# An adaLN block with linear attention and a GEGLU FFN: the 1/den broadcast loads dealt over two DMA queues, and the w_mod loads of the second gate placed behind the KV transposes

## The chip, the cores and the metric

One core of a Trainium2 chip runs the whole kernel. The metric is device microseconds (us) of one execution, as the median over several runs. The kernel before takes 805.02 us (three runs, 804.95 to 805.1).

The core has a matmul engine (PE, with its weight loads listed apart as PEld), a vector engine (DVE), a scalar engine (ACT), GpSimd (POOL), and a sync engine (SP) that does nothing here but issue DMAs. A DMA issued from SP or from ACT stands in that engine's instruction stream: it waits there for its semaphores, and what is behind it in the stream waits too.

## The reference

The input x is 2048 x 1024 in bf16. Six modulation rows come from one matrix product; they scale and shift the two normalised inputs and gate the two branches.

```python
mod = (_silu(c) @ w_mod).reshape(c.shape[0], 6, 1, -1)
sa, ca, ga, sb, cb, gb = (mod[:, 0], ..., mod[:, 5])
h = _layernorm(x) * (1 + ca) + sa
x = x + ga * _A_ref(h, A_wqkv, A_wo)        # linear attention, 32 heads of 32
h = _layernorm(x) * (1 + cb) + sb
x = x + gb * _B_ref(h, B_w_gate, B_w_up, B_w_down)   # gelu(h@wg) * (h@wu) @ wd, F = 3584
```

In the attention, with `phi(t) = where(t > 0, t + 1, exp(t)) + 1e-6`:

```python
pq, pk = phi(q), phi(k)
kv  = einsum('bhsd,bhse->bhde', pk, v);  z = einsum('bhsd->bhd', pk)
num = einsum('bhqd,bhde->bhqe', pq, kv)
den = einsum('bhqd,bhd->bhq', pq, z)[..., None] + 1e-6
o = num / den          # then @ wo
```

## The kernel before, in words

The 2048 rows are 16 chunks of 128 rows, in 4 supergroups (`sg`) of 512 rows. The 32 heads are 8 groups `g` of 4 heads `k`; each head holds 32 of the 128 partitions. The work goes through these stages on PE:

- **K and Q** (lines 858 and 909, to about 128 us): products of the modulated input with the weights; ACT and DVE make `phi` of them.
- **M tiles** (`m_tile`, line 873, from 127.8 us). Values are never formed: `M = phi(k)^T x` is made instead, in 24 tiles numbered `n`, each about 2.3 us of PE. A group has three tiles; `mcp` on ACT copies each to `mb` (line 878). When a group is complete, `m_t(g)` transposes `mb` to `mtb` by a DMA from SP (line 678), and `kv_prod(g)` (line 891) multiplies that with the value weights. `w2_pair` then folds the output weights in. The groups 0 to 3 become complete with tiles 2, 5, 8 and 11, and their `kv_prod` comes after the tiles 6, 9, 12 and 15.
- **den and its inverse.** `den` (line 1201) makes the denominators of two supergroups; DVE inverts them (line 1207) and SP stores them to DRAM in `scr_rd` (line 1209). `rb_load(sg, (h,))` (line 1221) reads them back for the half `h` (256 rows) of a supergroup, spread from one row per head to that head's 32 partitions: four DMAs of 256 KB, one for each quarter `k` of the partitions, together 1 MB in `rb`. `pq_scale` (line 1234, DVE, four instructions per half) multiplies `phi(q)` with it.
- **The output product** (`wo_chunk`, line 1242, chunks 0 to 15 from 193.8 us), 16 matmuls of 0.216 us to a chunk. DVE adds it to x (lines 1251 and 1255); ACT and POOL make the second normalisation (`ln2_stats` and `ln2_rows`: two ACT passes per chunk, lines 649 and 637), and a DMA transpose from SP gives `h2a` and `h2b` (line 678). For chunks 2 to 13 the work beside a chunk is in a hand-written table `SLOT`: `rb_load(2, (0,))` in slot 2, `(2, (1,))` in 4, `(3, (0,))` in 5, `(3, (1,))` in 10. `wt_dma` loads the first FFN weights (line 1325), `x_dma` reloads rows of x (line 569).
- **The FFN** (lines 1411 and 1496) in two passes, from about 246 us to the end. It multiplies by sums and differences of operand blocks (`ss` on line 1366, `tp` on line 1386) that DVE makes.

Beside the M tiles DVE also makes modulation rows from w_mod. `mod_step`, three times to a tile, does one multiply-add: 48 of them read `wmst` (loads on line 572), then `gb_acc` does 16 for the last half of the second gate `gb`, which read `wmg`. `gb_load(j, q)` (line 761) loads `wmg`: 512 KB each, `j` the column block of 512 columns, `q` the half of the rows; there are two buffers, so `gb_load(1, q)` waits until DVE has read `gb_load(0, q)`.

Everything is first listed in program order; the order on PE and SP is that order. `reorder` then plans the order on DVE, ACT and POOL anew, with a table of costs and due times, for the stretch from the end of the first K products up to slot 2; after that the written order holds. Each DMA issuer has a number of semaphore lanes (`LANES`), used in turn; a DMA waits until the one before it on its lane has landed.

The load of one half, before:

```python
for k in range(HPG):
    made.append(sch.dma(Q, lambda e, h=h, k=k: e.dma_start(
        RB[i][32 * k:32 * (k + 1), h, :, :],
        scr_rd[sg, h, k:k + 1, :, :].to_broadcast([32, NG, HW])), ...
```

`Q` is SP's stream, `A` is ACT's, `NG` is 8 and `HW` is 256 values of 4 bytes. In DRAM the 8 rows of 1 KB are 64 bytes apart (`SGW // 2 + 16`).

Of the kernel before, what the change touches and what calls it, by code (L numbers as in the profile page):

```python
# [14 lines left out]
NSG = 4  # L15
CPG = NCH // NSG
SGW = P * CPG
NDC = D // P
NG = 8
HPG = 4  # L20
# [8 lines left out]
PE_, ACT_, DVE_, POOL_, SP_ = "PE", "ACT", "DVE", "POOL", "SP"  # L29
# [124 lines left out]
class Sched:  # L154


    LANES = {SP_: 8, POOL_: 4, ACT_: 2}

    def __init__(self):
        self.streams = {e: [] for e in ENGS}  # L160
# [35 lines left out]
    def dma(self, stream, fn, rd=(), wr=(), deps=(), note="", overwrite_ok=False):  # L196
        nl = self.LANES[stream]
        k = self.lane_rr.get(stream, 0)
        self.lane_rr[stream] = (k + 1) % nl
        lane = f"{stream}q{k}"  # L200
        dd = list(deps)
        prev = self.lane_last.get(lane)
        if prev is not None:
            dd.append(prev)
        o = self.op(stream, fn, rd=rd, wr=wr, deps=dd, dma_lane=lane, note=note, overwrite_ok=overwrite_ok)
        self.lane_last[lane] = o
        return o
# [106 lines left out]
def bass_adaLN_cond__linear_attn_block__geglu_ffn__prompt_kernel(  # L314
# [12 lines left out]
    bf16, f32, f32r, i32 = dt.bfloat16, dt.float32, dt.float32r, dt.int32  # L327
    scr_row = nc.dram_tensor("scr_row", [3, 4, 512], f32).ap()
    scr_mod = nc.dram_tensor("scr_mod", [2, NDC, P], f32).ap()
    scr_rd = nc.dram_tensor("scr_rd", [NSG, 2, HPG, NG, SGW // 2 + 16], f32).ap()[:, :, :, :, 0:SGW // 2]  # L330
    with ExitStack() as es:
        es.enter_context(nc.allow_non_contiguous_dma(reason="1024 modulation values, laid out by partition"))
        arena = es.enter_context(nc.sbuf_tensor("arena", [P, ARENA_BYTES], dt.uint8, align_bytes=64))
# [4 lines left out]
        def at(name, shape, dty, off):  # L338
            return nc.alloc_sbuf_tensor_at(name, shape, dty, offset=ABASE + off, align_bytes=4)
# [33 lines left out]
        RB = [at(f"rb{i}", [P, 2, NG, SGW // 2], f32, OFF_RB[i]) for i in range(2)]  # L373
# [6 lines left out]
        GBB = at("gbb", [P, D], f32, OFF_GBB)  # L380
# [40 lines left out]
        def r_sm(name):  # L421
            return [(SMO[name], SMO[name] + SMSZ[name], name)]
# [7 lines left out]
        def r_xs(c0, c1):  # L430
            return [t_ for c_ in range(c0, c1) for t_ in r_x(c_)]
# [30 lines left out]
        def r_h2(h, k0=0, k1=NDC, s0=0, s1=SGW):  # L462
            return r_t8(H2O[h], f"h2{'ab'[h]}", k0, k1, s0, s1)
# [37 lines left out]
        def r_rb(i, h, g0=0, g1=NG):  # L501
            return [(OFF_RB[i] + (h * NG + g0) * 1024, OFF_RB[i] + (h * NG + g1) * 1024, f"rb{i}")]
# [12 lines left out]
        R_GBB = [(OFF_GBB, OFF_GBB + 4096, "gbb")]  # L515
# [13 lines left out]
        sch = Sched()  # L529
        T, A, V, G, Q = PE_, ACT_, DVE_, POOL_, SP_  # L530
# [37 lines left out]
        def x_dma(c0, c1):  # L568
            return sch.dma(Q, lambda e: e.dma_start(XALL[:, c0:c1, :], x_v[:, c0:c1, :]), wr=r_xs(c0, c1), note=f"x{c0}")
# [123 lines left out]
        def h2ap(h, dc, s0, s1):  # L693
            return H2[h][:, dc, s0:s1]
# [20 lines left out]
        def sc2(dc):  # L715
            return CB1T[:, dc:dc + 1], SBT[:, dc:dc + 1], r_sm("cb1T") + r_sm("sbT")
# [8 lines left out]
        def mod2_act(h, c0=0, n=CPG, dc0=0, dc1=NDC):  # L725
            s0, s1 = c0 * P, (c0 + n) * P
            for dc in range(dc0, dc1):
                sA, sB, rs_ = sc2(dc)
                sch.op(A, lambda e, dc=dc, sA=sA, sB=sB: e.activation(h2ap(h, dc, s0, s1), h2ap(h, dc, s0, s1), ACTF.Identity, bias=sB, scale=sA),
                       rd=r_h2(h, dc, dc + 1, s0, s1) + rs_, wr=r_h2(h, dc, dc + 1, s0, s1), note=f"h2modb {h}.{dc}")  # L730
# [29 lines left out]
        def gb_load(j, q):  # L760
            sch.dma(Q, lambda e: e.dma_start(WMG[q][:], wm_v[:, 4 * q:4 * q + 4, (10 + j) * 512:(11 + j) * 512]), wr=r_wmg(q), note=f"wmg{j}.{q}")
# [6 lines left out]
        def gb_acc(j, dc):  # L768
            acc, rng = GA_[j]
            src, rs_ = WMG[dc // 4][:, dc % 4, :], r_wmg(dc // 4, dc % 4, dc % 4 + 1) + r_sm("silf")  # L770
            if dc == 0:
                sch.op(V, lambda e: e.tensor_scalar(acc[:, :], src, SILF[:, 0:1], None, op0=ALU.mult), rd=rs_, wr=rng, note=f"macc{6 + j}.0")
            else:
                sch.op(V, lambda e: e.scalar_tensor_tensor(acc[:, :], src, SILF[:, dc:dc + 1], acc[:, :], op0=ALU.mult, op1=ALU.add),
                       rd=rs_ + rng, wr=rng, note=f"macc{6 + j}.{dc}")
            if dc % 4 == 3 and j == 0:
                gb_load(1, dc // 4)

        def gb_hilo(j):
            acc, rng = GA_[j]  # L780
# [3 lines left out]
        o_gb = [None]  # L784
# [47 lines left out]
        def row_load(dst, rng, row, a0, note, o_):  # L832
            sch.dma(Q, lambda e: e.dma_start(dst[:, :].rearrange("p (a b) -> p a b", a=2),
                                             scr_row[row, a0:a0 + 2, :].rearrange("(o a) b -> o a b", o=1).to_broadcast([P, 2, 512])),
                    wr=rng, deps=[o_], note=note)
# [281 lines left out]
        for c_ in range(10, NCH):  # L1117
            b = seq.index(("k", c_ // 2 * 2, 0)) - (9 if c_ % 2 else 12)
# [6 lines left out]
        for c_ in range(8, NCH, 2):  # L1125
            b = seq.index(("k", c_, 0)) - 3
# [10 lines left out]
        for g in range(NG):  # L1137
            task(nk + g // 2, lambda g=g: sch.dma(Q, lambda e: e.dma_start(WV[:, g, :, :], wqkv_v[:, :, 2 * D + g * P:2 * D + (g + 1) * P]),
                                                  wr=r_wv(g), note=f"wv{g}"))
# [54 lines left out]
        HW = SGW // 2  # L1194
# [18 lines left out]
        o_rd = {}  # L1213
        rb_ops = {}

        def rb_load(sg, hs=(0, 1)):
            i = sg % 2
            for h in hs:
                made = []
                for k in range(HPG):  # L1220
                    made.append(sch.dma(Q, lambda e, h=h, k=k: e.dma_start(  # L1221
                        RB[i][32 * k:32 * (k + 1), h, :, :],
                        scr_rd[sg, h, k:k + 1, :, :].to_broadcast([32, NG, HW])),
                        wr=r_rb(i, h) if k == 0 else (), deps=made[0].deps if k else [o_rd[sg // 2]], note=f"rb{sg}.{h}.{k}"))
                rb_ops[sg, h] = made

        GH = [((0, 2), (2, 4)), ((4, 6), (6, 8))]

        def pq_scale(sg, h, gs):
            i, t0 = sg % 2, h * HW  # L1230
            for g0, g1 in gs:
                ap = PQ[sg][:, g0:g1, t0:t0 + HW]
                rng = r_pq(sg, g0, g1, t0, t0 + HW)
                sch.op(V, lambda e, ap=ap, i=i, h=h, g0=g0, g1=g1: e.tensor_tensor(ap, ap, RB[i][:, h, g0:g1, :], ALU.mult),  # L1234
                       rd=rng + r_rb(i, h, g0, g1), wr=rng, deps=rb_ops[sg, h], note=f"pqs{sg}.{h}.{g0}")
# [50 lines left out]
        for n, (g, k) in enumerate(tiles):  # L1286
            m_tile(g, k, n % 4, n % 2)
            if k == 2:
                m_t(g)
            for _ in range(3):  # L1290
                mod_step()
            if 2 <= n <= 9:
                wofold(n - 2)
            while pend and n > 1:
                wm_dma(*pend.pop(0))
            if n in (1, 2):
                gb_load(0, n - 1)
            for f in HOOK.get(n, "").split():
                hook_run(f)
        for i in range(4):  # L1300
# [21 lines left out]
        def wt_dma(u):  # L1322
            i, f0 = u % 2, u * 256
            for t, v_ in enumerate((wg_v, wu_v)):
                sch.dma(Q, lambda e, t=t, v_=v_: e.dma_start(WT[i][:, t, :, :], v_[:, :, f0:f0 + 256]), wr=r_wt(i, t, t + 1), note=f"wt{t} u{u}")
# [20 lines left out]
        ND2 = NDC // 2  # L1346
# [24 lines left out]
        def t_sum(u, k):  # L1371
            if k == 3:
                ap, rd = wq(u, 1, 1)
                for t in range(2):
                    sch.op(A, lambda e, t=t: e.activation(TP[3][:, t, :, :], ap[:, t, :, :], ACTF.Copy), rd=rd[t:t + 1], wr=r_tp(3, t, t + 1), note=f"brcp u{u}")
                return
            if k == 0:
                (in0, r0), (in1, r1) = wq(u, 0, 1), wq(u, 0, 0)
            elif k == 1:
                (in0, r0), (in1, r1) = wq(u, 1, 1), (T32[0], r_tp(0))  # L1380
            elif k == 2:
                (in0, r0), (in1, r1) = wq(u, 1, 1), wq(u, 0, 1)
            else:
                (in0, r0), (in1, r1) = wq(u, 1, 0), (T32[1], r_tp(1))
            for t in range(2):
                sch.op(V, lambda e, t=t: e.tensor_tensor(TP[k][:, t, :, :], in0[:, t, :, :], in1[:, t, :, :], ALU.subtract),  # L1386
                       rd=r0[t:t + 1] + (r1[t:t + 1] if len(r1) == 2 else [(r1[0][0] + t * 2048, r1[0][0] + (t + 1) * 2048, r1[0][2])]),
                       wr=r_tp(k, t, t + 1), note=f"tsum{k} u{u}")
# [123 lines left out]
        def cb1():  # L1512
# [6 lines left out]
                6: lambda: (mod2(0, 0, 2), x_dma(10, 12)),  # L1519
                7: lambda: (t_sum(0, 0), t_sum(0, 1), pq_scale(2, 1, GH[0] + GH[1]), x_dma(12, 14)),  # L1520
                8: lambda: mod2(0, 2, 2),
                9: lambda: (pq_scale(3, 0, GH[0] + GH[1]), t_sum(0, 3), mod2_act(1, 0, 2), mod2_act(1, 2, 2, ND2)),
                10: lambda: (t_sum(0, 4), t_sum(0, 2), rb_load(3, (1,)), x_dma(14, 16), row_load(GBB, R_GBB, 2, 0, "gbb", o_gb[0]), wt_dma(1)),
                11: lambda: None,
                12: lambda: (s_sum(0, 0, 0), mod2(1, 2, 2, 0, ND2)),
                13: lambda: (s_sum(0, 0, 1), s_sum(0, 1, 0), s_sum(0, 1, 1), pq_scale(3, 1, GH[0] + GH[1]), s_sum(0, 2, 0))}
# [142 lines left out]
```

## Time and profile before

| | |
|---|---|
| median of the runs | 805.02 us |
| profiled execution: its own time | 806.37 us |
| profiled execution: span from the first instruction to the last | 804.5 us |
| granted TensorE clock | 1.000 |
| PE, DVE, ACT, POOL busy | 792.9, 568.1, 303.1, 39.4 us |
| loads of `rb`: number, size, median from issue to landing | 32, 256 KB, 5.4 us |
| loads of `wmg`: number, size, median from issue to landing | 4, 512 KB, 6.0 us |
| transposes to `mtb`: number, median and longest to landing | 8, 5.1 and 10.3 us |

The profile shows one execution. An engine row in the timeline gives the start, the duration, the line and operation, the tiles written and read, and in brackets the idle time before it with what ended that idle time. Of an SP or ACT row of a DMA the duration is that of the issue, not of the transfer; the transfer lands later. A row of the windows gives, for a stretch of time, the busy time of each engine, the clock, the busy share of the 16 DMA engines and the rate in GB/s.

### The profile page before, as it was taken

What the parts mean: (1) busy time and instruction counts of PE and PEld (TensorE: products, weight loads), DVE (VectorE), ACT (ScalarE), POOL (GpSimd) and SP (SyncE); (2) the same over time, 40 slices, a digit from 0 to 9 for tenths busy, and PEclk for the clock granted to TensorE, in tenths of its full rate; (3) what the DMA queues carried; (4) which work ended last, traced back from release to release, by engine and by line L of the source; (5) the groups of instructions that cost most, each with busy time, mean ns of one, the idle gap of its engine ahead of it and who ended that gap; (6) DMA issues with size and microseconds to landing.
All of it is one profiled execution on the core that took longest, in us unless ns stands there. A gap on an engine that the chain in (4) does not pass through costs nothing.

```text
span 804.5 us, 10875 instructions
## 1 busy us (share of the span) xinstructions
PE 792.9 (99%) x4029; PEld 465.3 (58%) x4029; DVE 568.1 (71%) x1008; ACT 303.1 (38%) x511; POOL 39.4 (5%) x102
## 2 busy tenths in 40 slices
PE   7999999999999999999999999999999999999998
PEld 4444445666444677767775444467776777744445
DVE  6699898984699978788786375577887878601422
ACT  2497743232655444344443410033544435300000
POOL 2121200000320000000000000000000000000000
PEclk9999999999999999999999999999999999999999
DMA  9789859749898135323237324022231323430100
GB/s 282 242 176 231 176 116 230 186 98 184 186 265 225 53 112 150 98 61 104 58 101 235 53 74 110 20 86 76 82 105 53 106 72 86 136 126 7 53 20 27
DMA packets 168508, 97.73 MB, mean 121 GB/s; under 512 B 68476, under 2 KB 156804, under 8 KB 168456
## 3 DMA queue, kind: packets, MB, share of 16 engines
q1 hardware_dynamic: 168440, 97.04, 47.0%
q8 instruction: 32, 0.52, 0.3%
q14 instruction: 20, 0.16, 0.1%
q10 hardware_dynamic: 16, 0.00, 0.0%
HBM read 78.92 MB, written 4.47 MB: 104 GB/s over the span
## 4 chain that ended last, share of the span: by engine, by line
PE 84%; DMA 6%; SPq 4%; DVE 3%; issue 1%; ACT 1%; POOL 0%; DVEq 0%; POOLq 0%; ACTq 0%
PE ps_all L1411 43%; PE ps_all L1496 24%; PE ps_all L909 7%; PE ps_all L858 6%; PE ps_all L873 3%; DMA rb<-scr_rd 3%; DMA mtb<-mb 1%; SPq L575 1%; DVE pq L1234 1%; DMA wmq<-in_w_mod_dram 1%; SPq L580 1%; DVE ss L1366 1%; SPq L1221 1%; DMA scr_row<-mrowa 1%; SPq L678 1%
## 5 line engine op out<-in xcount | busy, mean ns | idle before, releaser
L1411 PE MATMUL ps_all<-ss,tp 128*128 128x512 f32 x896 | 224.7, 402 | 1.2 <-DVE ss L1366 1.2
L1496 PE MATMUL ps_all<-wd,yT 128*128 128x512 bf16 (+3 forms) x952 | 193.9, 366 | 0.0
L1411 PEld LDWEIGHTS ps_all<-ss,tp 128*128 128x128 f32 x896 | 168.2, 188 | 42.4 <-DVE ss L1366 2.6
L1496 PEld LDWEIGHTS ps_all<-wd,yT 128*128 128x128 bf16 x952 | 90.0, 98 | 103.8 <-ACT ge L1427 0.5
L1427 ACT ACTIVATE ge<-ps_all 128x512 f32<-128x512 f32 x112 | 64.2, 597 | 144.7 <-DVE ps_all L1422 79.7
L1411 PE MATMUL ps_all<-h2a,wt 128*128 128x512 bf16 x448 | 106.2, 380 | 0.4 <-DVE xall L1255 0.4
L1386 DVE TENSOR_TENSOR tp<-wt 128x512 fp32r<-128x512 bf16 x112 | 74.3, 688 | 39.6 <-PE ps_all L1411 20.8
L1431 DVE TENSOR_TENSOR yT<-ge,ps_all 128x512 bf16<-128x512 f32 x112 | 74.7, 685 | 34.4 <-PE ps_all L1411 31.0
L1422 DVE TENSOR_TENSOR ps_all<-ps_all,es 128x512 f32<-128x512 f32 x112 | 75.3, 696 | 16.1 <-PE ps_all L1411 16.1
L1488 DVE TENSOR_TENSOR ps_all<-ps_all,gbb 128x512 f32<-128x512 f32 (+3 forms) x34 | 22.7, 668 | 79.0 <-PE ps_all L1496 79.0
L1386 DVE TENSOR_TENSOR tp<-wt,tp 128x512 fp32r<-128x512 bf16 x112 | 72.0, 684 | 0.0
L1411 PEld LDWEIGHTS ps_all<-h2a,wt 128*128 128x128 bf16 x448 | 39.4, 98 | 55.0 <-issue 14.8
L1242 PE MATMUL ps_all<-w,pq 128*128 128x512 bf16 x256 | 56.5, 379 | 1.6 <-DVE pq L1234 1.6
L858 PE MATMUL ps_all<-wk,h1T 128*128 128x512 bf16 x248 | 56.8, 379 | 0.3 <-DVE h1T L699 0.2
L909 PE MATMUL ps_all<-h1T,wq 128*128 128x512 bf16 x256 | 56.7, 379 | 0.0
L1411 PE MATMUL ps_all<-ar,tp 128*128 128x512 f32 x224 | 55.3, 389 | 0.0
L1416 ACT ACTIVATE ps_all<-ps_all 128x512 f32<-128x512 f32 x56 | 32.6, 582 | 53.2 <-PE ps_all L1411 51.4
L847 ACT ACTIVATE eb<-ps_all 128x512 f32<-128x512 f32 x64 | 36.4, 594 | 37.7 <-PE ps_all L858 15.6
L1411 PEld LDWEIGHTS ps_all<-ar,tp 128*128 128x128 f32 x224 | 42.0, 188 | 8.7
L1242 PEld LDWEIGHTS ps_all<-w,pq 128*128 128x128 bf16 x256 | 24.7, 98 | 32.0 <-DVE pq L1234 2.3
L909 PEld LDWEIGHTS ps_all<-h1T,wq 128*128 128x128 bf16 x256 | 24.9, 98 | 30.0
L1419 ACT ACTIVATE es<-ps_all 128x512 f32<-128x512 f32 x56 | 33.5, 601 | 18.6 <-PE ps_all L1411 18.6
(118 smaller groups left out, 638.0 us busy)
## 6 DMA issues: line engine op xcount, KB each, us to landing
wt<-in_B_w_gate_dram SPq DMA_DIRECT2D x28, 512.0 KB, 4.2
wt<-in_B_w_up_dram SPq DMA_DIRECT2D x28, 512.0 KB, 4.9
wd<-in_B_w_down_dram SPq DMA_DIRECT2D x12, 1024.0 KB, 7.3
rb<-scr_rd SPq DMA_DIRECT2D x32, 256.0 KB, 5.4
wmst<-in_w_mod_dram SPq DMA_DIRECT2D x6, 1024.0 KB, 5.6
wmq<-in_w_mod_dram SPq DMA_DIRECT2D x8, 512.0 KB, 6.1
out_dram<-xall SPq DMA_DIRECT2D x31, 128.0 KB, 1.7
xall<-in_A_x_dram SPq DMA_DIRECT2D x5, 512.0 KB, 4.1
```

The source lines that it names most:

```text
L847: sch.op(A, lambda e: e.activation(EB[i][:, :], PS(bank), ACTF.Exp), prd=pr(bank), wr=rng, note=f"{note}.exp")
L858: o = sch.op(T, lambda e, dc=dc: e.matmul(PS(bank), H1[sg][:, ci, dc, :], W_[:, dc, jg * 512:(jg + 1) * 512], start=(dc == 0), stop=(dc == ...
L909: o = sch.op(T, lambda e, dc=dc: e.matmul(PS(b), WQ[:, dc, qc * P:(qc + 1) * P], H1[sg][:, :, dc, :], start=(dc == 0), stop=(dc == NDC - 1 ...
L1242: last[half] = sch.op(T, lambda e, g=g, half=half: e.matmul(PS(b0 + half), PQ[sg][:, g, ci * P:(ci + 1) * P], W2[:, g, half * 512:(half + ...
L1386: sch.op(V, lambda e, t=t: e.tensor_tensor(TP[k][:, t, :, :], in0[:, t, :, :], in1[:, t, :, :], ALU.subtract), rd=r0[t:t + 1] + (r1[t:t + ...
L1411: o = sch.op(T, lambda e, l_=l_, r_=r_, dc=dc: e.matmul(PS(b), l_, r_, start=fresh and dc == 0, stop=dc == ND2 - 1, skip_group_check=True) ...
L1416: sch.op(A, lambda e: e.activation(PS(BB + t), PS(BA + t), ACTF.Copy), prd=pr(BA + t), pwr=pr(BB + t), note="pcp")
L1419: sch.op(A, lambda e: e.activation(ES[t][:, :], PS(BE + t), ACTF.Copy), prd=pr(BE + t), wr=r_2k(OFF_ES[t], f"es{t}"), note="escp")
L1422: sch.op(V, lambda e: e.tensor_tensor(PS(dst + t), PS(BB + t), ES[t][:, :], ALU.add), prd=pr(BB + t), rd=r_2k(OFF_ES[t], f"es{t}"), pwr=pr ...
L1427: sch.op(A, lambda e: e.activation(GE[i][:, :], PS(b), ACTF.Gelu_apprx_tanh), prd=pr(b), wr=r_2k(OFF_GE[i], f"ge{i}"), note="gelu")
L1431: sch.op(V, lambda e: e.tensor_tensor(YT[:, yrow(fc), h * SGW:(h + 1) * SGW], GE[i][:, :], PS(b + 1), ALU.mult), rd=r_2k(OFF_GE[i], f"ge{i ...
L1496: o = sch.op(T, lambda e, fc=fc: e.matmul(PS(b, 0, n), YT[:, yrow(fc), ci * P:(ci + 1) * P], WDT[fc // 4][:, fc % 4, c0:c1], start=first a ...
```

## The change

It does five things.

1. The four quarter loads of each half of `rb` are issued in the order k = 0, 2, 1, 3, with 0 and 1 from SP and 2 and 3 from ACT, instead of 0, 1, 2, 3 from SP.
2. The padding of 64 bytes behind each 1 KB row of `scr_rd` goes, and both sides of a load are written as one run of 8 KB per partition.
3. ACT gets 8 semaphore lanes for its DMAs instead of 2.
4. `gb_load(0, 0)` and `(0, 1)` move from the M tiles 1 and 2 to the tiles 6 and 7. `gb_load(1, 0)` and `(1, 1)`, issued before as soon as `gb_acc` had listed the last read of each buffer (in tiles 10 and 11), both come at the end of tile 11, behind the transpose of group 3.
5. `rb_load(3, (1,))` moves from the middle of slot 10 to the head of slot 9.

```diff
-    LANES = {SP_: 8, POOL_: 4, ACT_: 2}
+    LANES = {SP_: 8, POOL_: 4, ACT_: 8}
...
-    scr_rd = nc.dram_tensor("scr_rd", [NSG, 2, HPG, NG, SGW // 2 + 16], f32).ap()[:, :, :, :, 0:SGW // 2]
+    scr_rd = nc.dram_tensor("scr_rd", [NSG, 2, HPG, NG, SGW // 2], f32).ap()
...
-            if dc % 4 == 3 and j == 0:
-                gb_load(1, dc // 4)
...
-                for k in range(HPG):
-                    made.append(sch.dma(Q, lambda e, h=h, k=k: e.dma_start(
-                        RB[i][32 * k:32 * (k + 1), h, :, :],
-                        scr_rd[sg, h, k:k + 1, :, :].to_broadcast([32, NG, HW])),
-                        wr=r_rb(i, h) if k == 0 else (), deps=made[0].deps if k else [o_rd[sg // 2]], note=f"rb{sg}.{h}.{k}"))
+                for k in (0, 2, 1, 3):
+                    made.append(sch.dma((Q, A)[k // 2], lambda e, h=h, k=k: e.dma_start(
+                        RB[i][32 * k:32 * (k + 1), h, :, :].rearrange("p a b -> p (a b)"),
+                        scr_rd[sg, h, k:k + 1, :, :].rearrange("k g t -> k (g t)").to_broadcast([32, NG * HW])),
+                        wr=r_rb(i, h) if not made else (), deps=made[0].deps if made else [o_rd[sg // 2]], note=f"rb{sg}.{h}.{k}"))
...
-            if n in (1, 2):
-                gb_load(0, n - 1)
+            if n in (6, 7):
+                gb_load(0, n - 6)
+            if n == 11:
+                gb_load(1, 0)
+                gb_load(1, 1)
...
-                9: lambda: (pq_scale(3, 0, GH[0] + GH[1]), t_sum(0, 3), mod2_act(1, 0, 2), mod2_act(1, 2, 2, ND2)),
-                10: lambda: (t_sum(0, 4), t_sum(0, 2), rb_load(3, (1,)), x_dma(14, 16), row_load(GBB, R_GBB, 2, 0, "gbb", o_gb[0]), wt_dma(1)),
+                9: lambda: (rb_load(3, (1,)), pq_scale(3, 0, GH[0] + GH[1]), t_sum(0, 3), mod2_act(1, 0, 2), mod2_act(1, 2, 2, ND2)),
+                10: lambda: (t_sum(0, 4), t_sum(0, 2), x_dma(14, 16), row_load(GBB, R_GBB, 2, 0, "gbb", o_gb[0]), wt_dma(1)),
```

## The prediction

> **What bounds the kernel now.** I read the page's busy times first, then what PE waited for after the start, then the timelines of PE, DVE and SP around each wait.
>
> ```profile
> PE 792.9 (99%) x4029; PEld 465.3 (58%) x4029; DVE 568.1 (71%) x1008; ACT 303.1 (38%) x511; POOL 39.4 (5%) x102
> ```
>
> PE is busy for 792.9 of 804.5 us, so no edit outside PE's own work can give more than 11.6 us. What it waits for from 27 us on:
>
> ```profile
> PE ps_all L1242 <- DVE pq L1234: 1.6, 1, 1.6
> PE ps_all L1411 <- DVE ss L1366: 1.2, 3, 0.7
> PE ps_all L891 <- DMA mtb<-mb: 1.1, 1, 1.1
> PE ps_all L1411 <- DVE xall L1255: 0.4, 1, 0.4
> ```
>
> That is 4.3 us in all, and it is the ceiling of this change: its loads start after 127 us. Two rows of PE's timeline place the larger waits:
>
> ```profile
> 153.58 0.62 PE L891 MATMUL ps_all<-mtb,wv 128*128 128x128 bf16 x8 [1.11 <-DMA mtb<-mb]
> 231.87 13.99 PE L1242 MATMUL ps_all<-w,pq 128*128 128x512 bf16 x64 [1.59 <-DVE pq L1234]
> ```
>
> For the first, SP's timeline:
>
> ```profile
> 136.83 0.42 SPq L761 DMA_DIRECT2D wmg<-in_w_mod_dram  x1
> 137.35 1.28 SPq L678 DMA_TRANSPOSE mtb<-mb  x1
> 138.73 0.52 SPq L572 DMA_DIRECT2D wmst<-in_w_mod_dram  x1
> 139.30 3.31 SPq L761 DMA_DIRECT2D wmg<-in_w_mod_dram  x1
> 142.71 0.45 SPq L572 DMA_DIRECT2D wmst<-in_w_mod_dram  x1
> 143.26 9.25 SPq L678 DMA_TRANSPOSE mtb<-mb  x2
> ```
>
> The transpose of group 1 is issued at 143.26 and lands 10.3 us later (the longest of its kind; the median is 5.1), behind two `wmg` and two `wmst` loads, 3 MB. For the second wait, DVE's timeline:
>
> ```profile
> 220.73 2.50 DVE L1234 TENSOR_TENSOR pq<-pq,rb 128x512 bf16<-128x512 bf16 x4 [3.00 <-DMA rb<-scr_rd]
> 231.12 2.50 DVE L1234 TENSOR_TENSOR pq<-pq,rb 128x512 bf16<-128x512 bf16 x4 [1.14 <-DMA rb<-scr_rd]
> ```
>
> DVE stood 3.00 and 1.14 us for the two halves of `rb` of supergroup 2. From 231.12 until the FFN runs it is never idle for long, and the small PE waits on `ss` and `xall` (0.44, 0.72, 0.17 and 0.30 us between 246 and 259) are the end of that DVE chain. So the end moves with the landing of the second half, at 231.0. Why these loads are slow is in the windows:
>
> ```profile
> 144.00:150.00 6.00, 6.00 (x48) 4.05 (x46) 6.00 (x8) 1.17 (x4) 0.00 (x0) 1.00 1.10 348
> 197.00:206.00 9.00, 9.00 (x49) 4.22 (x48) 2.17 (x5) 2.05 (x2) 0.19 (x1) 1.00 1.09 218
> 137.60:139.00 1.40, 1.40 (x12) 0.94 (x10) 1.37 (x4) 1.03 (x3) 0.00 (x0) 1.00 1.06 234
> ```
>
> In the first only w_mod loads move (128 partitions, rows of 1 KB): 348 GB/s. In the second only `rb` (32 partitions to a DMA, rows of 1 KB): 218, with the DMA engines as busy. The row length is the same, so it is the 32 partitions or the repeated source. The third is `gab`, a row of 4 KB spread to all 128 partitions: 234.
>
> **The change part by part.**
>
> **First-gate-half loads behind the transpose.** `gb_load(0, .)` leaves the queue ahead of group 1's transpose: 1 MB, at 348 GB/s 3.0 us. The transpose lands at about 150.5 instead of 153.5; PE wants it at 152.47. The wait of 1.11 us goes, with 1.9 us to spare. The other end is no gain, if the first `wmst` transfer still holds the queue. What the loads now stand before: the transpose of group 2. It was ready for PE by 155 at the latest, and its product starts at 161.44; 3.0 us more is covered. The first DVE read of `wmg` is at 158.90; issued near 144.5 and landing after 9.0 (its longest), the load is there at 153.5. I take 1.1.
>
> **Second-block loads behind group 3's transpose.** `gb_load(1, 0)` stood at 163.44, waiting for DVE's fourth `gb_acc`, and group 3's transpose went out behind it at 163.92. Now the transpose goes first; PE took its result at 169.93 without a wait. Nothing is gained. Behind the two loads stand the row store of 169.12 and later the store of 1/den, as the second load did before. Taken at 0.
>
> **The planner.** With other SP positions it may order DVE and ACT differently from 27 us on. PE has no wait there now except the one above; one DVE instruction moved ahead of another costs at most a `wofold` (1.15 us) either way. Taken at 0, bounds -1.2 and +1.2.
>
> **The quarter loads.** SP issues two instead of four to a half, at 0.45 us: 0.9 us less on SP. ACT issues two: 0.9 us by SP's median, 1.2 by the one ACT issue in the trace (0.585). Supergroup 0 and 1: `rb` was not the last wait of PE there (DVE waited 0.51 and 1.74, but PE ran on), so 0. Supergroup 2, first half: issued at 213.13, landed at 220.7, 7.55 us, of which 1 MB at 218 GB/s is 4.8. ACT's two loads follow its normalisation pass that ends at 211.7, so they have 1.4 us of lead. If the two queues together make 348, about 0.49 MB is moved by the lead and 1.6 us remain: landing 213.1 + 2.7 + 1.6 = 217.4. At 234 it is 218.9. DVE is free at 217.73. Its wait of 3.0 falls to between 0 and 1.2.
>
> Second half: from there DVE has 2.4 (`pq_scale`) + 1.1 + 2.1 + 1.2 + 2.5 us of work, so its next `pq_scale` could start near 227.5 to 228.5. In the queues, before the last byte of this half, lie 1 MB of `rb` for each of the two halves, 1 MB of `wt` (3.6 us at 295 GB/s, the rate of the window from 253 to 255, where `wt` moves), three transposes (3.8 us by their issue rows of 1.25), and now half a megabyte for supergroup 3 that ACT sends early. 2.5 MB of `rb` take 7.5 us at 348 GB/s and 11.2 at 234. ACT's first load goes at 211.7; the fixed part is 2.7 less 0.9 for two issues, 1.8. The landing is 211.7 + 1.8 + 3.6 + 3.8 + 7.5 = 228.4, or 232.1 at 234, which is no earlier than now. I take 229.0, nearer to 348, because the same 1 KB rows reach it in the first window, while 234 comes from a window of 1.4 us that holds one transfer's ramp. So DVE's chain starts 2.1 us earlier than 231.12 (bounds 0 and 2.7), and PE's waits of 1.59 + 1.63 = 3.2 fall to 1.1.
>
> [...]
>
> **ACT's own cost.** Its pairs of issues fall before chunk passes that had idle time ahead of them: 1.19 us before the pass at 212.89, 0.53 before 218.70, 1.11 before 222.19, 3.01 before the modulation at 239.92, where the pair moved to slot 9 stands. SP's position of that load does not change. The cost is at most 0.6 us in one place, and idle times of 1.49 and 3.50 follow it. In the planned stretch a pair waits for the store of 1/den (landed near 178.8); ACT's idle times there are 1.9 to 3.4 us between copies, and PE has four banks. Taken at 0; below nothing it cannot be.
>
> **Lanes.** No wait in SP's list is one for a lane, and 17 ACT DMAs on 8 lanes have none either. 0.
>
> Sum: 1.1 + 2.1 = 3.2 us. Against the profiled execution: 806.37 - 3.2 = 803.2 (804.5 - 3.2 = 801.3 of span and 1.9 around it). That execution is 1.35 above the median, so the median becomes 805.02 - 3.2 = 801.8. The ceiling of 4.3 gives 800.7.
>
> **The rivals.**
>
> *The two queues share the rate.* The `rb` landing stays near 231 and only group 1's transpose pays: 805.02 - 1.1 = 803.9, or 805.0 if that fails too. For it: the DMA engines' share is already 1.1 to 1.2 from 213 to 257 us, and `gab`, which reaches all partitions, has only 234. Against it: 348 at the same share. The part of the range within 0.2% of now is 803.4 to 806.6.
>
> *ACT stands in its queue.* Slower. An issue can last: SP's `wt` issue at 217.27 took 3.01 us, and one `mtb` issue 5.1. If ACT's issues of rb 2.1, 3.0 and 3.1 are held like these, ACT loses 9 to 15 us between 211 and 240. Its slack before the modulation of `h2b` is 3.50 + 0.33 + 3.01 = 6.8; what is over it goes to PE. It decides from 2.6 us to a pair on (6.8 + 1.1 regained, over three pairs). Price: 15.4 - 6.8 - 1.1 = 7.5, so 806 to 812.5. Against it: SP's own 32 `rb` issues took 1.65 at most, and ACT's queue holds nothing else.
>
> **How the numbers follow.** A measurement of this kernel tells about 0.2%, 1.6 us, from no change. Faster by both mechanisms: 0.66, 800.7 to 803.4. Shared rate, within 0.2%: 0.17. ACT held, or a worse plan: 0.17, over 806.6. The range of 800.5 to 806.6 takes in the first two and a little below the ceiling for the spread of runs.
>
> **What would show it.** Right: no bracket on the `mtb` product near 152; `rb` windows between 211 and 230 above 218 GB/s; DVE's waits of 3.00 and 1.14 gone or small; PE idle after 27 us at 1 to 1.5 us. Wrong: ACT issue rows of over 2 us with ACT passes late behind them; `rb` windows still at 218 to 234; a new PE wait on `mtb` of groups 2 to 7 or on `mb`.

## The result, and the profile after

The changed kernel is slower. In runs beside each other it takes 816.74 us (four runs, 815.91 to 820.35) and the kernel before 804.99 us (four runs, 804.64 to 805.1): a ratio of 1.0155, with a 95% interval of 1.0125 to 1.0186. The profiled execution took 816.61 us, of which 814.4 are its span, at a mean granted clock of 0.992. Against the profiled execution before that is 10.2 us more in time and 9.9 us more in span.

The page's busy times of the kernel after. PE is busy 2.9 us longer with the same 4029 matmuls, and it idles more:

```profile
PE 795.8 (98%) x4029; PEld 466.4 (57%) x4029; DVE 568.3 (70%) x1008; ACT 303.5 (37%) x511; POOL 38.2 (5%) x102
```

What PE waited for from 27 us on (total, times, longest):

```profile
PE ps_all L1240 <- DVE pq L1232: 9.3, 1, 9.3
PE ps_all L889 <- DMA mtb<-mb: 2.3, 1, 2.3
PE ps_all L1412 <- DVE ss L1367: 0.3, 1, 0.3
```

The 4.3 us of before have become 11.8 (9.31 + 2.25 + 0.28 in the timeline's rows). PE's timeline shows where they stand (start, duration, and in brackets the idle time before the row with what ended it):

```profile
151.37 0.61 PE L889 MATMUL ps_all<-mtb,wv 128*128 128x128 bf16 x8
...
199.59 0.62 PE L889 MATMUL ps_all<-mtb,wv 128*128 128x128 bf16 x8 [2.25 <-DMA mtb<-mb]
...
200.48 3.50 PE L1240 MATMUL ps_all<-w,pq 128*128 128x512 bf16 x8
...
241.43 15.71 PE L1240 MATMUL ps_all<-w,pq 128*128 128x512 bf16 x64 [9.31 <-DVE pq L1232]
```

The product of group 1 at 151.37 has no bracket any more: that wait of 1.11 us went. M tiles also began 0.9 us earlier (126.83 for 127.76); the lead was there at 25.20, where the last `wmq` product began (before: 26.14), and the start varies among the profiled executions below (126.86 to 128.49). The output product began at 191.55, 2.2 us earlier than before. Then come two new waits, each with a tail. The 8 matmuls at 200.48 took 3.50 us where they took 1.89 before, and the 64 from 241.43 took 15.71 where they took 13.99. The windows show why (busy times by engine, the granted clock as the third number from the right, DMA share, GB/s): after each wait the clock stands at half.

```profile
201.00:203.00 2.00, 2.00 (x6) 0.68 (x5) 0.00 (x0) 0.70 (x1) 0.00 (x0) 0.50 0.98 197
...
241.00:243.00 2.00, 1.57 (x4) 0.58 (x5) 2.00 (x4) 1.47 (x3) 0.52 (x2) 0.50 0.97 192
243.00:245.00 2.00, 2.00 (x6) 0.76 (x5) 2.00 (x6) 1.73 (x2) 0.99 (x3) 0.51 1.21 306
```

The account: 11.84 - 4.33 = 7.5 us of waiting, 1.6 + 1.7 = 3.3 of slow matmuls, less 0.9 of the earlier start. That is 9.9, the difference of the spans.

The wait of 9.31 us is the main loss. Its cause is read backwards. DVE's timeline: the `pq_scale` of the second half of supergroup 2 started at 240.68, against 231.12 before, and its idle time ended with an `rb` load.

```profile
223.25 2.50 DVE L1232 TENSOR_TENSOR pq<-pq,rb 128x512 bf16<-128x512 bf16 x4 [3.68 <-DMA rb<-scr_rd]
...
240.68 2.50 DVE L1232 TENSOR_TENSOR pq<-pq,rb 128x512 bf16<-128x512 bf16 x4 [1.57 <-DMA rb<-scr_rd]
```

SP's timeline says why that load came late. SP's share of it was issued at 231.27; before, the load stood at 223.12. It stood behind a transpose whose issue lasted 9.74 us.

```profile
217.53 1.23 SPq L678 DMA_TRANSPOSE h2a<-xl  x1
...
221.43 9.74 SPq L678 DMA_TRANSPOSE h2a<-xl  x1
231.27 2.16 SPq L1219 DMA_DIRECT2D rb<-scr_rd  x2
233.53 3.29 SPq L678 DMA_TRANSPOSE h2a<-xl  x1
```

The longest issue of an `h2a` transpose before was 2.64 us, in the same place:

```profile
220.38 2.64 SPq L678 DMA_TRANSPOSE h2a<-xl  x1
```

A long issue alone is not new: the prediction's list has 9.25 us for two `mtb` transposes in SP's queue before, behind w_mod loads, but there the windows stood at 348 GB/s. ACT's timeline shows ACT's shares of the loads going out early and quickly, in about a microsecond to a pair, beside SP's transposes, and then two normalisation passes that stand for 6.25 and 6.60 us until a transpose has landed and freed their buffer:

```profile
217.77 1.00 ACTq L1219 DMA_DIRECT2D rb<-scr_rd  x2
...
223.08 0.83 ACTq L1219 DMA_DIRECT2D rb<-scr_rd  x2
...
229.17 1.15 ACT L649 ACTIVATE xl<-xall,mv 128x1024 bf16<-128x1024 bf16 x1 [6.25 <-DMA h2a<-xl]
...
238.15 1.15 ACT L649 ACTIVATE xl<-xall,mv 128x1024 bf16<-128x1024 bf16 x1 [6.60 <-DMA h2a<-xl]
```

The windows of that stretch show DMA engines that count as busy and move little:

```profile
220.00:222.00 2.00, 2.00 (x11) 0.87 (x9) 0.00 (x0) 1.47 (x4) 0.43 (x3) 1.00 1.43 125
222.00:224.00 2.00, 2.00 (x11) 0.91 (x10) 0.75 (x2) 0.91 (x1) 1.11 (x4) 1.00 0.99 97
224.00:226.00 2.00, 2.00 (x11) 0.94 (x10) 2.00 (x4) 0.00 (x0) 0.00 (x0) 1.00 0.97 91
226.00:228.00 2.00, 2.00 (x11) 0.89 (x10) 0.89 (x2) 0.00 (x0) 0.00 (x0) 1.00 1.23 112
```

91 to 125 GB/s. The same four windows before:

```profile
220.00:222.00 2.00, 2.00 (x11) 0.94 (x10) 1.27 (x3) 1.07 (x1) 1.66 (x4) 1.00 1.01 247
222.00:224.00 2.00, 2.00 (x11) 0.90 (x10) 2.00 (x4) 1.81 (x3) 0.44 (x3) 1.00 1.20 290
224.00:226.00 2.00, 2.00 (x11) 0.88 (x9) 2.00 (x9) 0.56 (x1) 0.84 (x3) 1.00 1.22 293
226.00:228.00 2.00, 2.00 (x11) 0.92 (x10) 2.00 (x5) 1.95 (x3) 0.47 (x2) 1.00 1.14 209
```

And the `h2a` transposes, which before landed 3.1 us (median) and at most 5.6 us after their issue:

```profile
DMA to landing us min/median/max: 3.1/7.7/16.6
```

So the reading of the trace is: a DMA transpose in SP's queue and plain loads in ACT's queue, in flight together, hold each other up; the transpose is stuck, what stands behind it on SP is late, and so are the passes that wait for its landing. It is only a reading until one cause at a time is taken away.

### The profile page after: what moved, and what is told of

Its sections match the earlier page's. It is cut to its first block, busy times and chain, and to the rows that moved or that the text cites. A ratio compares the mean times of both kernels' runs of the same rounds, so it can differ in the third digit from the quotient of the medians.

```text
span 814.4 us, 10888 instructions
## 1 busy us (share of the span) xinstructions
PE 795.8 (98%) x4029; PEld 466.4 (57%) x4029; DVE 568.3 (70%) x1008; ACT 303.5 (37%) x511; POOL 38.2 (5%) x102
## 4 chain that ended last, share of the span: by engine, by line
PE 89%; SPq 4%; DMA 3%; DVE 2%; issue 1%; ACT 1%; POOL 0%; ACTq 0%; DVEq 0%; POOLq 0%
PE ps_all L1412 42%; PE ps_all L1497 24%; PE ps_all L871 7%; PE ps_all L907 7%; PE ps_all L856 6%; SPq L678 3%; PE ps_all L1240 1%; DMA mtb<-mb 1%; DMA h2b<-xl 1%; DMA wmq<-in_w_mod_dram 1%; DVE ss L1367 1%; SPq L1219 0%; PE ps_all L889 0%; PE ps_all L1172 0%; PE ps_all L742 0%
## 5 line engine op out<-in xcount | busy, mean ns | idle before, releaser
L1240 PE MATMUL ps_all<-w,pq 128*128 128x512 bf16 x256 | 59.8, 395 | 9.3 <-DVE pq L1232 9.3
L856 PEld LDWEIGHTS ps_all<-wk,h1T 128*128 128x128 bf16 x248 | 23.6, 98 | 28.9 <-DVE h1T L699 2.4
```

Source lines behind the costliest of these rows:

```text
L856: o = sch.op(T, lambda e, dc=dc: e.matmul(PS(bank), H1[sg][:, ci, dc, :], W_[:, dc, jg * 512:(jg + 1) * 512], start=(dc == 0), stop=(dc == ...
L1240: last[half] = sch.op(T, lambda e, g=g, half=half: e.matmul(PS(b0 + half), PQ[sg][:, g, ci * P:(ci + 1) * P], W2[:, g, half * 512:(half + ...
```

## The experiments

The theory: the loss comes from ACT's queue running beside SP's transposes. The rivals: the new form of the loads (8 KB rows without the padding) is what disturbs the transposes, whichever queue issues it; the moved `gb` loads are at fault; ACT's early loads only put their bytes ahead of the transposes; or ACT pays by standing in its own queue, as the prediction's rival had it. Ratios are to the kernel before on the same chip, with 95% intervals.

**All four loads from SP again.** Against the kernel after:

```diff
-sch.dma((Q, A)[k // 2], ...
+sch.dma(Q, ...
```

> The changed kernel, with all four quarter loads of 1/den issued from SP (order 0, 2, 1, 3, rows of 8 KB), so that no second queue runs beside the transposes. Theory Q (transposes on SP's queue starve while ACT's queue moves the loads on the same DMA engines): about 801 to 804 us, the transpose to h2a that took 9.7 us to issue back under 3, no PE wait of 9 us. Theory R (rows of 8 KB alone are the trouble, on whatever queue): as slow as the changed kernel, 814 to 818. Theory G (the moved w_mod loads): 814 to 818.

Measured: 803.98 us, 0.9989 (0.9979 to 0.9999). It keeps the 8 KB rows, the `gb` moves and all else, and is 12.8 us faster than the kernel after. SP's timeline and the windows of the stretch, and PE's row of chunk 10:

```profile
217.80 2.76 SPq L678 DMA_TRANSPOSE h2a<-xl  x1
220.66 1.91 SPq L1219 DMA_DIRECT2D rb<-scr_rd  x4
```

```profile
218.00:220.00 2.00, 2.00 (x11) 0.93 (x10) 1.72 (x3) 1.11 (x1) 1.70 (x3) 1.00 1.21 302
220.00:222.00 2.00, 2.00 (x11) 0.94 (x10) 2.00 (x5) 1.06 (x2) 0.77 (x2) 1.00 1.20 287
```

```profile
229.22 13.99 PE L1240 MATMUL ps_all<-w,pq 128*128 128x512 bf16 x64 [0.90 <-DVE pq L1232]
```

The transpose is back at 2.76 us, the rate at about 290 GB/s, the wait at 0.90. With all else as it was, the dealing makes the loss; 8 KB rows in SP's own queue do not.

This run also weighs the rival of the bytes put ahead. From the start of the first `h2a` transpose to the end of the third one's issue the kernel after moved 143 GB/s for 17.55 us (213.62 to 231.17), 2.51 MB; this kernel moved 208 GB/s for 10.74 us (209.82 to 220.56), 2.23 MB. The 0.28 MB more would take 1.3 us at 208 GB/s, an estimate; the stretch is 6.8 us longer. So most of the delay is the rate and a small part is the order of the bytes.

**Dealt, but in rows of 1 KB.** The kernel after with the padding of `scr_rd` and the three-dimensional load of before, still from two queues:

```diff
-        RB[i][32 * k:32 * (k + 1), h, :, :].rearrange("p a b -> p (a b)"), ...to_broadcast([32, NG * HW])
+        RB[i][32 * k:32 * (k + 1), h, :, :], ...to_broadcast([32, NG, HW])
```

> The changed kernel, dealt over SP and ACT as it is, but with the rows of 1/den left as 1 KB with 64 bytes between them, as before. Theory Q in its form 'a transpose packet of 256 bytes waits each time for one packet of the other queue': the wait is 8 times shorter, so most of the loss is gone, 801 to 806 us. Theory Q in its form 'two queues beside a transpose, of whatever packet': 812 to 818. Theory R: about 802.

Measured: 808.9 us, 1.005 (1.0033 to 1.0066). From SP's and PE's timelines:

```profile
219.23 8.04 SPq L678 DMA_TRANSPOSE h2a<-xl  x1
```

```profile
235.87 15.59 PE L1240 MATMUL ps_all<-w,pq 128*128 128x512 bf16 x64 [5.22 <-DVE pq L1232]
```

Still slower than before, by 4 us instead of 12, and between the two forms of the theory that I had set down. The 256 bytes of the first form are in the trace: while the transpose of 221.43 was being issued, the kernel after moved 736 packets of 256 bytes in SP's queue and 61 of 8 KB in ACT's. That the one waits for the other each time is shown by no row. The dealing does the harm with either row, and more of it with the long one: over the 803.98 us of the kernel with all loads on SP (in 8 KB rows; none was run with 1 KB rows) it costs 4.9 us with 1 KB rows and 12.8 with 8 KB.

**The `gb` moves alone**, on the kernel before:

```diff
-            if dc % 4 == 3 and j == 0:
-                gb_load(1, dc // 4)
...
-            if n in (1, 2):
-                gb_load(0, n - 1)
+            if n in (6, 7):
+                gb_load(0, n - 6)
+            if n == 11:
+                gb_load(1, 0)
+                gb_load(1, 1)
```

> The kernel before, with only the w_mod loads of the second gate moved. My step for it: the wait of 1.1 us on mtb near 152 us goes, about 803.9 us. Theory G (these loads are what makes the change slow, through the transposes of groups 2 to 7): 812 or more. Planner rival: 806 to 808 with new waits between 27 and 193 us.

Measured: 804.69 us, 0.9997 (0.9988 to 1.0006). In its profiled execution the wait at 152 is gone and the output product begins at 191.58 (before 193.77; 0.9 us of that is the earlier start of the M tiles, 126.86), but the wait for the second half of `rb` grew from 1.59 to 2.00, and the 64 matmuls behind it took 15.67 instead of 13.99 us, at a granted clock of 0.57:

```profile
230.03 15.67 PE L1240 MATMUL ps_all<-w,pq 128*128 128x512 bf16 x64 [2.00 <-DVE pq L1232]
```

```profile
230.00:234.00 4.00, 3.97 (x11) 1.52 (x12) 4.00 (x9) 3.59 (x5) 1.10 (x3) 0.57 1.13 209
```

So earlier work met a load that comes when it comes. That profiled execution took 805.19 us with a mean clock of 0.998. Eight of the ten runs had 1.000, with a median of 804.58 against 805.04 before, so the clock explains the profiled execution and not the whole of the missing 1.1 us. The rest is open.

**The dealt loads without the `gb` moves**, the kernel after with point 4 of the change undone:

> The changed kernel, with the w_mod loads of the second gate put back where they were before; the loads of 1/den stay dealt in rows of 8 KB. Theories Q and R: the loss stays, 815 to 819 us. Theory G: 801 to 805.

Measured: 815.38 us, 1.0133 (1.0112 to 1.0153). The longest transpose issue is 10.76 us (SP's timeline), the wait before chunk 10 is 9.60.

```profile
219.76 10.76 SPq L678 DMA_TRANSPOSE h2a<-xl  x1
```

With the previous run this settles the parts: the `gb` moves are worth little either way, and the dealt loads carry the loss.

**Dealt, but never beside a transpose.** Each transpose waits for ACT's last loads to land, and ACT's loads wait for the last transpose:

```diff
+            d_ += rb_act                                  # before every transpose
...
-  deps=made[0].deps if made else [o_rd[sg // 2]]
+  deps=[o_rd[sg // 2]] + ([last_t[0]] if k // 2 else [])
+                rb_act[:] = [made[1], made[3]]
```

The edit does one thing more: three of the four loads of a half no longer wait for the last reader of their buffer, as `made[0].deps` had them do.

> The changed kernel, with two waits added: a transpose waits until ACT's last two quarter loads have landed, and a quarter load on ACT waits until the transpose before it has landed. Same bytes, same queues, same rows of 8 KB, but a transpose and ACT's loads never share the DMA engines. Theory Q (it is the sharing that collapses the rate): faster than the changed kernel in spite of the waits, 804 to 811 us, and the transpose issue of 9.7 us back under 3. Theory B (ACT's early loads only take their bytes' time ahead of the transposes): slower than the changed kernel, 817 to 822.

Measured: 824.08 us, 1.0228 (1.0212 to 1.0244), outside what I expected in total: by its time alone the run speaks for theory B. Its rows speak for the sharing. SP's timeline gives 3.29 us for the transpose that took 9.74, the other `h2a` issues are 1.23 to 1.46 in this stretch, and the wait before chunk 10 fell from 9.31 to 4.84 us (PE's timeline, first row):

```profile
225.63 3.29 SPq L680 DMA_TRANSPOSE h2a<-xl  x1
```

```profile
237.47 16.04 PE L1243 MATMUL ps_all<-w,pq 128*128 128x512 bf16 x64 [4.84 <-DVE pq L1235]
...
265.45 3.59 PE L1415 MATMUL ps_all<-h2a,wt 128*128 128x512 bf16 x8 [6.73 <-ACT ps_all L1420]
```

The second row shows what I had left out: a load that waits in ACT's stream holds ACT's copies behind it, and the FFN's start pays 6.73 us for that and another 3.31 for an `xall` row. It is the price that the prediction's rival described, made by my own wait. Because of it the run does not show what the sharing costs in time; the transpose also waited before its issue, so its short row alone is no proof. The comparison of bytes and rates under the first experiment is the stronger one against theory B.

**Other traffic on ACT's queue.** If the cause is a second queue beside transposes, it need not be `rb`. This takes the kernel of the first experiment, with all `rb` loads from SP, and issues the first two weight loads of the FFN (512 KB, rows of 512 bytes) from ACT:

```diff
-sch.dma(Q, lambda e, t=t, v_=v_: e.dma_start(WT[i][:, t, :, :]
+sch.dma(A if u == 0 and not wt_n else Q, ...
```

> The kernel of e1_sp_only (804.0 us, loads of 1/den all from SP), with the first two FFN weight loads (wt, 2 x 512 KB, rows of 512 bytes, all 128 partitions) issued from ACT instead of SP, so that they move beside the transposes of the chunks 1 to 3. Theory Q, any traffic of a second queue beside a transpose: the transposes near 217 to 223 us take 5 us or more to issue, 807 to 812. Theory P (it takes the large packets of the 1/den rows): 803 to 805.

Measured: 807.23 us, 1.0027 (1.0016 to 1.0038), against 803.98 with the same loads from SP. ACT's, SP's and PE's timelines:

```profile
211.82 0.43 ACTq L1328 DMA_DIRECT2D wt<-in_B_w_gate_dram  x1
```

```profile
214.21 9.60 SPq L678 DMA_TRANSPOSE h2a<-xl  x2
```

```profile
224.79 8.57 PE L1240 MATMUL ps_all<-w,pq 128*128 128x512 bf16 x32 [2.62 <-DVE pq L1232]
```

Two transposes took 9.60 us to issue together (the longer 6.78), with plain weights of short rows on the other queue, so a long issue needs no broadcast there. It is not the same collapse, though: from 214 to 224 us the rate was 211 GB/s (162 to 248 in windows of 2 us). And PE's wait came another way: the first half of `rb`, sent by SP at 211.92 ahead of both transposes, landed near 224, and DVE stood 7.51 us for it. The weights went out 2.8 us earlier than in the first experiment (211.82 for 214.66), beside that `rb` load instead of behind it, so how much of the 3.2 us is their bytes ahead and how much the second queue is not shown.

**Which loads.** Only the loads of supergroups 2 and 3 dealt, those of 0 and 1 from SP:

```diff
-sch.dma((Q, A)[k // 2], ...
+sch.dma((Q, A if sg > 1 else Q)[k // 2], ...
```

> The changed kernel, dealt over two queues only for the supergroups 2 and 3; those of 0 and 1 all from SP. By the profile the wait of 9.3 us before chunk 10 comes from the former and the wait of 2.3 us on mtb of group 7 (with the clock drop after it, some 2 us) from the latter: 811 to 814 us expected, and the mtb wait gone. If the early ones alone did it: 804.

Measured: 813.52 us, 1.0096 (1.0081 to 1.0111). The wait on `mtb` of group 7, which had been 2.25 us, is gone; in the kernel after, ACT's loads of supergroup 1 went out at 189.62 and 191.75, beside the transpose of 191.80. The wait before chunk 10 stays, so it belongs to the loads beside the `h2a` transposes:

```profile
235.96 16.45 PE L1240 MATMUL ps_all<-w,pq 128*128 128x512 bf16 x64 [7.18 <-DVE pq L1232]
```

**All from SP, and early.** If the load's place is what counts, the place can be had without a second queue. Both loads of supergroup 2 right behind the reload of x near 200 us, ahead of the `h2a` transposes:

```diff
         x_dma(NXR, 10)
+        rb_load(2)
...
-                2: (pq_scale(1, 0, GH[0] + GH[1]), rb_load(2, (0,)))
+                2: pq_scale(1, 0, GH[0] + GH[1])
-                4: (cb1(), rb_load(2, (1,)))
+                4: cb1()
```

> The kernel of e1_sp_only, with both loads of 1/den of supergroup 2 issued right behind the reload of x near 200 us instead of in the slots 2 and 4, when the queue is nearly empty until 209 us. If the landing of these loads is what PE waits for, its waits of 0.9, 0.4, 0.7, 0.2 and 0.3 us go: 801.5 to 802.5 us. If DVE's chain is bound by its own work: 803.5 to 804.5.

Measured: 801.59 us, 0.9952 (0.994 to 0.9965): faster than both kernels. What PE waited for after 27 us is one line of 0.2 us, and while `rb` moves alone the windows have about the rate of before (218 there):

```profile
PE ps_all L1413 <- DVE ss L1368: 0.2, 1, 0.2
```

```profile
197.00:203.00 6.00, 6.00 (x36) 2.90 (x34) 0.39 (x2) 2.05 (x2) 0.00 (x0) 1.00 1.03 236
```

SP's timeline of this fast kernel has a long transpose issue too, two of them in 7.37 us (the longer 3.81), behind eight loads of its own queue:

```profile
210.25 7.37 SPq L678 DMA_TRANSPOSE h2a<-xl  x2
```

PE waits for nothing that stands behind them here, so a long issue alone was no loss in this kernel.

**Dealt where I took the queue to be free of transposes.** The early version with the loads of supergroups 1 and 2 dealt, and then with those of 2 alone:

```diff
-sch.dma(Q, ...
+sch.dma((Q, A)[k // 2] if sg in (1, 2) else Q, ...     # second kernel: if sg == 2
```

> The kernel of e8_early (801.6 us), with the loads of 1/den of the supergroups 1 and 2 dealt over SP and ACT; in that kernel they move between 195 and 215 us, where no transpose is in flight, and those of 0 and 3 stay on SP. Theory Q (dealing hurts only beside transposes): 801 to 802.5 us, no PE wait above 1 us. Theory D (two queues lose rate whatever runs beside them): 804 or more.

Measured: 802.77 us, 0.9974 (0.9963 to 0.9985), and what PE waited for:

```profile
PE ps_all L889 <- DMA mtb<-mb: 2.1, 1, 2.1
```

My assumption was wrong for supergroup 1: ACT ran ahead and sent those loads at 190.15, beside the last `mtb` transpose. It is the same 2 us as in the kernel after.

> The kernel of e8_early (801.6 us), with only the loads of supergroup 2 dealt over SP and ACT; they move after the reload of x and before the first chunk transposes. In e11_dealt_clear ACT's loads of supergroup 1 went out at 190 us beside the transpose of group 7 after all, and PE waited 2.1 us for it. Theory Q (sharing with a transpose is the damage): 801.3 to 802.2 us and no PE wait above 0.5. Theory D (two queues cost by themselves): 803 or more.

Measured: 801.73 us, 0.9963 (0.9951 to 0.9976), with no PE wait over 0.3 us after 27 us. The dealt loads went out between 198.79 and 202.48 us, and SP issued no transpose between those of 192.40 and 210.06. Here two queues did no harm; they did no good either (801.59 from one queue).

**What limits a load of 32 partitions.** Three kernels with one run each; in all of them the multiplier is not 1/den but rows of the FFN's down weights, so that the source can be varied. First, the early version in which each load reads 32 different runs of 8 KB instead of one run 32 times:

> The kernel of e8_early, with the 32 partitions of each 1/den load reading 32 different runs of 8 KB (of w_down) instead of all the same one; the scaling of phi(q) is therefore another. A look at the rate between 196 and 215 us, 229 to 250 GB/s in e8_early. If the 32 partitions of a load are the limit, as my prediction had it: unchanged, 220 to 260. If it is the repeated source: 330 to 390.

Second, the same with supergroups 1 and 2 dealt:

> As e9_distinct (32 different runs of 8 KB, the scaling is another), with the loads of the supergroups 1 and 2 dealt over SP and ACT by quarter, 0 and 1 on SP, 2 and 3 on ACT. If the partitions are the limit, the two queues reach the two halves at once: 330 to 400 GB/s where both run, against 220 to 260 on SP alone. If the source is: 330 to 390 in both. In e5_excl, with the repeated source and both queues at once, some 240.

Third, the first with one load of 128 partitions to a half (1 MB) instead of four of 32:

```diff
-for k in (0, 2, 1, 3):  ... 32 rows of 8 KB to RB[i][32 * k:32 * (k + 1), h]
+for k in (0,):          ... 128 rows of 8 KB to RB[i][:, h]
```

> As e9_distinct (different runs of 8 KB of w_down, the scaling is another), with one load over all 128 partitions for each half instead of four over 32. A look at the rate between 196 and 213 us. If the 32 partitions of a load are what holds it at 229 to 250 GB/s: 330 to 400 here. If it is the packet of 8 KB or the 4-byte type: 220 to 260.

Measured: 800.6, 802.47 (with a wait of 1.6 us on `mtb` again) and 800.5 us. The windows of the three kernels, in this order, in stretches where their loads move:

```profile
207.00:213.00 6.00, 6.00 (x29) 2.74 (x28) 6.00 (x10) 4.41 (x6) 2.69 (x7) 1.00 1.03 235
```

```profile
207.00:213.00 6.00, 6.00 (x30) 2.73 (x28) 6.00 (x12) 2.86 (x4) 3.30 (x8) 1.00 1.01 240
```

```profile
197.00:199.00 2.00, 2.00 (x17) 1.17 (x16) 0.29 (x1) 0.45 (x1) 0.00 (x0) 1.00 1.02 406
199.00:201.00 2.00, 1.95 (x10) 0.92 (x10) 0.00 (x0) 0.93 (x2) 0.00 (x0) 1.00 0.99 391
201.00:203.00 2.00, 2.00 (x11) 0.81 (x9) 0.62 (x1) 0.68 (x1) 0.00 (x0) 1.00 1.00 367
203.00:205.00 2.00, 2.00 (x11) 0.90 (x10) 2.00 (x5) 0.92 (x1) 0.22 (x1) 1.00 1.04 438
```

Different source rows: 235 instead of 236 GB/s. Two queues: 240. One load over all partitions: 367 to 438, at the same DMA share (a reload of x, over 128 partitions too, moves among them). A second queue with the other half of the partitions doesn't lift the rate. That the 32 partitions of a load set it is the likely reading, and not fully shown: the last kernel's loads are also four times as large. The FFN's weight loads before, 512 KB over 128 partitions, stood at 295 in the prediction's window, which speaks for the partitions. The time did not follow the rate: 800.5 against 800.6 us.

## Why the prediction was wrong

I forecast 801.8 us with 0.66 on faster and gave 0.17 to slower; the time is 816.74, 10 us above the top of the range.

**The step that failed: "The quarter loads".** Its sum put three transposes in at "their issue rows of 1.25", 3.8 us, next to loads in another queue. Measured, the three took 2.74, 1.23 and 9.74 us, 13.7 in all, and `pq_scale`, which waits for the second half of `rb`, started at 240.68 and not near 229.0. The rows of before were misread as well: the three that stand ahead of that load are 1.25, 1.24 and 2.64, 5.1 us, and two `mtb` transposes behind plain loads had taken 9.25. No row of before showed a transpose beside a second busy queue, and I did not bound that cost, as one must for a thing that the trace does not show. Undoing the dealing gives back 12.8 us and the rate (208 for 143 GB/s over the stretch); dealing supergroup 2 away from transposes costs nothing (801.73 against 801.59). This much is shown. How a transpose and another queue's packets hold each other up inside the DMA engines is not: only that little moved (91 to 125 GB/s at a share of 0.97 to 1.43), that the third transpose took 9.74 us to issue against 2.76 in the same place with all the loads on SP, and that 8 KB rows cost more than 1 KB rows (12.8 us for 4.9).

**The rate in the same step.** I took 348 GB/s for two queues, reasoning that 1 KB rows reach it elsewhere and that 234 was a transfer's ramp. No run shows 348 for loads of 32 partitions, from one queue or two, and none that the 234 was a ramp: that the two halves of the partitions would run side by side from two queues was not shown, and 240 from two queues is against it. The 32-partition loads stay at 235 to 240 from one queue or two, with repeated source rows or different ones; a load of 128 had 367 to 438. Even without the stall the step would have given nothing: it is my "shared rate" rival, and dealing supergroup 2 away from transposes measured 801.73 against 801.59.

**"First-gate-half loads behind the transpose": right.** The row at 151.37 has no bracket, and in the kernel with that move alone it has none either. Worth 1.1 as a wait removed; in time that kernel's ratio is 0.9997. What I missed is what is late next: PE arrives about 2 us earlier at the second half of `rb` (0.9 of it from the start of the M tiles), whose landing did not move as much, so its wait grew from 1.59 to 2.00.

**"Second-block loads", "The planner", "Lanes": right** in that no wait appeared on `mtb` of group 3 or a lane. The M tiles' start, 0.9 us earlier, is not the plan's doing: the lead stood at 25.20 us, before the planned stretch, and the dealt kernel without the `gb` moves began them at 128.49, 0.7 us later than before.

**"ACT's own cost": right as far as it went.** ACT's 16 issues of `rb` took 0.31 to 1.15 us each. The rival "ACT stands in its queue" gave the right sign for a reason that did not occur: its sign, rows of over 2 us, is absent. ACT did stand, 6.25 and 6.60 us, but in passes that waited for transposes to land.

**A term that was missing: the clock.** I counted a wait as its own length. Here the two long waits (2.25 and 9.31 us) left 3.3 us of slow matmuls behind them, at a granted clock of 0.50 to 0.51.

The last sign that I listed for "wrong", a new PE wait on `mtb` of groups 2 to 7, did appear (group 7). I had named the place and not the mechanism.

## What to carry to other kernels

Before moving loads to a second queue, look at what the first one carries: if there are DMA transposes in it, the loads' gain is not the question but the transposes' delay (here up to 9.74 us of issue for 2.76), and everything that stands behind them (here 12.8 us in all). If loads are late, try issuing them earlier in the same queue (here 0.5% faster than before) before adding a queue. A load over more partitions moved faster here (367 to 438 GB/s for 235), without a gain in time. A part of a sum that no row shows needs a price from both sides, also when it is not what is being changed: here the neighbour in the other queue.

## What the runs showed that was not expected

- **A short wait cost more than itself.** PE waits of 0.90 and 1.59 us before chunk 10 left the 64 matmuls behind them at 13.99 us. Waits of 2.00, 5.22, 7.18 and 9.31 were followed by 15.59 to 16.45 us for the same 64. Windows show a granted clock near 0.5 for three of them: those of 1 us have 0.79, 0.50, 0.50 and 0.51 from 230 on after the wait of 2.00, the window from 234 to 238 has 0.52 with that of 7.18, and the one from 241 to 243 has 0.50 after that of 9.31. The length does not decide alone: in the kernel with the transposes kept apart a wait of 3.31 us left the 8 matmuls behind it at their usual 1.89 and the clock at 1.00. So 2.00 was enough in one execution, and 3.31 was not in another.
- **A second queue did not lift the rate, a load over 128 partitions did:** 235 to 240 GB/s for loads of 32 partitions and 256 KB, 367 to 438 for 128 and 1 MB, with the DMA engines' share at 0.99 to 1.04 in all. A share near 1 therefore says little about how fast the data moves; in the stall it stood at 0.97 with 91 GB/s.
- **Longer rows cost more here.** Beside transposes, dealt rows of 8 KB cost 12.8 us (816.74 against 803.98), rows of 1 KB 4.9 (808.9), and one megabyte of weights in rows of 512 bytes 3.2 (807.23). The amounts of data and the places of the loads differ, so this is an order and not a law.
